# Block products added by accumulating transfers, a ring of product units, and a rearranged first block in a fused convolution and feed-forward kernel

## The chip, the cores and the metric

The kernel runs on one core of one Trainium2 chip. The core has five engines with a queue each, in order: TensorE (PE: matmuls, which write PSUM), VectorE (DVE), ScalarE (ACT), GpSimd (POOL) and SyncE (SP, which here issues nearly all transfers). The metric is the device time of one execution in microseconds (us). In the profile, PEld is PE's weight load.

## The reference, cut to what matters

```
def A(q, k, v, shift_k, ssm_k, ssm_D):            # S = 2048, D = 640, bf16
    k_shift = sum over t<4 of k shifted by t along S, times shift_k[:, t]
    kv = k_shift * v
    y  = irfft(rfft(kv padded to 2S) * rfft(ssm_k padded to 2S))[:S]   # causal convolution along S
    y  = y + kv * ssm_D
    return q * y
def B(x): return (silu(x @ w_gate) * (x @ w_up)) @ w_down              # F = 1728
h   = x + A(layernorm(x), k, v, ...)              # x = A_q
out = h + B(layernorm(h))
```

## The kernel before

**Tiling.** The sequence is cut in four blocks of 512 rows (i = 0..3). The causal convolution becomes a sum over block pairs: block i of the spectrum is the sum over j <= i of X[j] * C[i-j], where X[j] is the transform of block j of kv and C[m] that of parts of the convolution kernel, combined by `kcomb`. So block 1 has two products, block 2 three, block 3 four.

**Stages of block i.** `kv`: kT is loaded transposed, the four taps run as matmuls on PE (L543, L548; 64-row and 64-column tiles with the tap weights on a diagonal), ACT copies the result back into kT (L554), five DMA transposes turn it to kvo, and DVE multiplies it into vt (L563). `xfwd` (via `halves`): 32 matmuls with cosine and sine tables (L502), ACT evicts them (L514), DVE butterflies (L491) make X. `prod(j, i)`: for each half f2 two DVE multiplies of 2560 elements (L576, L577) into the temporary tt, one subtraction and one addition (L579, L581) and, for j > 0, one addition into the sum Y (L584). After the last j, butterflies give IO and IE. `inverse`: 32 matmuls (L637); then, per column group j of 0..3, ACT adds a bias while it evicts (L648), DVE multiplies (L650), ACT sums and sums squares (L652, L654), POOL makes the norm's factor with a power (L656, L658), DVE scales (L660) and a DMA transpose brings the result to hnT. `ffn`: 13 full slots of gate and up matmuls (L681, L682: 10 each) and a half-filled slot (L692), in which gate and up take 64 rows each; ACT evicts with Silu and Copy (L699, L701), DVE multiplies to gu or gz (L703); then the down matmuls of each j (L715, 14 slots by two halves; gz's first 64 rows are zeros) and DVE's last addition (L721) before the store. Before that, kc is transposed on PE (L477) and copied by ACT (L482) to KT, and `kfwd` transforms it; for kf0 DVE evicts half of it with the butterfly in one operation (L510). The first norm of x is `ln1`: for block 0 by DVE's statistics (L598, L599), for others by ACT (L607, L610); ACT applies it (L622).

**Order.** Every operation is recorded with `add` as a task with a number; `schedule` takes a written order of these numbers for each engine (ORDER) and gives out four PSUM units of two banks each, and `emit` makes the waits. So nothing is reordered on the chip, and a wait holds all that stands behind it on its engine. IO shares its place with kT, and IE with hnT.

Of the kernel before, what the change touches and what calls it, by code (L numbers as in the profile page):

```python
# [10 lines left out]
ALU = mybir.AluOpType  # L11
ACTF = mybir.ActivationFunctionType
P = 128
# [10 lines left out]
class _Task:  # L24
    __slots__ = ("eng", "fn", "cost", "lat", "deps", "after", "succ", "npred", "ready", "end", "start",
                 "opens", "tiles", "idx", "clock", "sem", "seq", "dma", "name", "gap")


class _Tile:
# [8 lines left out]
    def f(self, b, n, parts=slice(0, P)):  # L38
        o = self.unit * 1024 + b * 512
        return self.g.ps[parts, o:o + n]  # L40

# [13 lines left out]
class _Graph:  # L55


    def __init__(self, nc, es, units=4):
        self.nc = nc
        self.es = es  # L60
        self.tasks = []
        self.lastw = {}
        self.readers = {}
        self.units = units
        self.ps = es.enter_context(nc.psum_tensor("ps", [P, 4096], dt.float32))
        self.psb = self.ps[:].bitcast(dt.bfloat16)
# [26 lines left out]
    def add(self, eng, name, fn, cost, r=(), w=(), pr=(), pw=(), skip=(), lat=None, dma=None, after=()):  # L93
# [4 lines left out]
        t.after = set(after)  # L98
        t.opens = None
        t.tiles = []  # L100
        t.gap = 0.0
        t.seq = len(self.tasks)
# [34 lines left out]
    def schedule(self, order):  # L137
# [17 lines left out]
        pipe = 0.0  # L155
        self.glob = []
        while len(self.glob) < len(self.tasks):
            best = None
            for e in ENGINES:
# [3 lines left out]
                s = max(free[e], t.ready)  # L163
                if t.opens is not None:
# [11 lines left out]
            if t.opens is not None:  # L176
                pt = t.opens
                u = min((u for u in range(self.units) if unit_by[u] is None), key=lambda u: unit_free[u])
                pt.unit = u
                left[pt] = len(pt.users)  # L180
                t.deps.update(last_users.get(u, ()))
                unit_by[u] = pt
            free[e] = s + t.cost
            t.end = s + t.cost + t.lat
# [19 lines left out]
    def emit(self, block):  # L204
# [5 lines left out]
        for t in self.glob:  # L210
            kn = known[t.eng]
            waits = {}
            merged = []
            for d in t.deps:
# [64 lines left out]
    """,  # L279
    "act": """  # L280
# [10 lines left out]
    """,  # L291
    "dve": """
# [10 lines left out]
    """,  # L303
    "pool": """
        8 5 6 7 147 148 149 150 151 204 205 196 220 197 221 212 213 327 328 329 408 409 400 384 401 392 385 393 506 507 508 581
        597 582 598 589 573 590 574 695 696 697 780 796 781 797 772 773 788 789
    """,
    "sp": """
# [7 lines left out]
def bass_sequential_preLN__ssm_conv_h3__swiglu_ffn__prompt_kernel(  # L316
# [31 lines left out]
    ftab_d = nc.inline_tensor(_to_bf16(np.stack([np.cos(angx), np.sin(angx)], 1).reshape(P, -1)), name="cst_ftab")  # L348
    itab_d = nc.inline_tensor(_to_bf16(np.stack([np.cos(angi), np.sin(angi)], 1).reshape(P, -1)), name="cst_itab")
# [4 lines left out]
    with ExitStack() as es:  # L354
# [16 lines left out]
        Y = sb("Y", S[6], [4, 2, D])  # L371
# [10 lines left out]
        tt = sb("tt", o, [2, 2, 2, D])  # L382
        t1, t2 = tt[:, 0], tt[:, 1]
        tacc = bass.AP(t1.tensor, t1.offset, [list(t1.ap[0]), [2 * D, 2], [5 * D, 2], [1, D]])
# [9 lines left out]
        jk = sb("jk", o + 15360, [D])  # L394
        ub = [sb("ub%d" % i, o + 16640 + 1024 * i, [N]) for i in range(2)]
        gz = sb("gz", o + 18688, [N])
        o += 19712
# [13 lines left out]
        KO = [sb("KO%d" % m, p, [2, 2, D]) for m, p in enumerate((w + 10240, S[4], w + 10240, S[4] + 5120))]  # L411
        o = w + 17920
# [4 lines left out]
        mv = [sb("mv%d" % i, o + 320 + 32 * i, [4], f32) for i in range(4)]  # L417
# [3 lines left out]
        BN, DIRECT = (0,), ('kf0',)  # L421
# [26 lines left out]
        load("ftab", ftab[:], ftab_d.ap().rearrange("p (a j c) -> p a j c", a=2, j=4), 524288)  # L448
        load("itab", itab[:], itab_d.ap().rearrange("p (a f j c) -> p a f j c", a=2, f=2, j=4), 524288)
# [5 lines left out]
        g.add("pool", "gz", lambda e: e.memset(gz[0:H, :], 0.0), 500, w=[gz[0:H, :]])  # L455
# [36 lines left out]

        def halves(cls, name, src, ev, od, scale, direct=False):
# [23 lines left out]
        def kfwd(m, dst):  # L517
            halves("kf", "kf%d" % m, KT[m], dst, KO[m], D ** 0.5 / N, "kf%d" % m in DIRECT)
            for f in range(0 if "kf%d" % m in DIRECT else 2):
                bfly("kf%d" % m, dst[:, f], KO[m][:, f], dst[:, f], dst[:, f + 2], 2 * D)  # L520

        def kcomb(dst, own, prev, m):
# [3 lines left out]
                  cdve(4 * D), r=[own[:, :, 1, :], prev[:, :, 0, :]], w=[dst[:, :, 1, :]])  # L526

        def kv(i):
# [6 lines left out]
            for a in range(3):  # L535
# [17 lines left out]
                ks = kT[:, c0:c0 + nb, 0:N]  # L553
                g.add("act", nm, lambda e, pt=pt, ks=ks, nb=nb: e.activation(  # L554
# [5 lines left out]
            for lo, src, n, k in ((0, 0, P, 3), (P, P + H, H, 2), (P + H, P, H, 2)):  # L560
# [4 lines left out]
        def xfwd(i):  # L565
            halves("xf", "xf%d" % i, vt, XH[i], FO, 1.0, "xf%d" % i in DIRECT)
            for f in range(0 if "xf%d" % i in DIRECT else 2):
                bfly("xf%d" % i, XH[i][:, f], FO[:, f], XH[i][:, f], XH[i][:, f + 2], 2 * D)

        def prod(j, i):  # L570
# [228 lines left out]
```

## Time and profile before

| | |
|---|---|
| median of 3 runs (lowest to highest) | 274.79 us (273.31 to 275.04) |
| the profiled execution: its own time | 276.58 us |
| span of the profile | 274.6 us |
| mean granted PE clock | 0.981 |
| PE busy | 255.8 us (93%) |
| DVE busy | 210.5 us (77%) |
| ACT busy | 187.9 us (68%) |
| POOL busy | 37.8 us (14%) |
| chain that ended last | PE 58%, DVE 25%, ACT 9%, DMA 6% |
| DVE: L576 and L577 | 20 each, 29.7 us each |
| DVE: L584 | 12 of 2560 elements, 17.8 us |

The page splits the span in 40 slices of 6.9 us; a digit is the busy share in tenths. Matmuls overlap in their records: a PE that is shown busy is not at its peak, and the pace is read from start to start. A row of the timeline gives start, duration, engine, line, operation, output and inputs, the count, and in brackets the idle time ahead with what ended it. In a row of stages each engine has its busy time in that stretch and, in brackets, its instructions; the last three columns are the granted PE clock, the DMA engines' share and GB/s.

### The profile page before, as it was taken

How to read it: one execution, taken by the hardware profiler on the slowest of the kernel's cores; microseconds unless marked ns; L12 is line 12 of the kernel's file. 1: busy time of each engine (PE TensorE's matmuls, PEld its weight loads, DVE VectorE, ACT ScalarE, POOL GpSimd, SP SyncE). 2: the span in 40 equal slices, each digit the busy share in tenths (PEclk: the TensorE clock that was granted, in tenths of full speed). 3: DMA queues.
4: the chain of work that ended last, by engine and by line, in shares of the span. 5: the costliest groups of instructions: out<-in, count | busy, mean ns of one | idle time of the engine just before them, and what ended most of it. 6: DMA issues, size and time to landing. Idle time of an engine off the chain costs nothing.

```text
span 274.6 us, 4036 instructions
## 1 busy us (share of the span) xinstructions
PE 255.8 (93%) x1596; PEld 143.4 (52%) x1596; DVE 210.5 (77%) x281; ACT 187.9 (68%) x338; POOL 37.8 (14%) x54
## 2 busy tenths in 40 slices
PE   0998767899899999999999999999999999999995
PEld 0566434354544566754444666644446774444673
DVE  1479997987999999999999999999999413212222
ACT  1798998989966799167978892667769911546400
POOL 1002302900040011100040054000500220000000
PEclk9999989599999999999999999999999999999999
DMA  7999974274900073463100415530000050200002
GB/s 171 318 175 319 381 272 98 48 118 102 376 17 0 0 169 85 94 170 114 46 1 2 98 21 124 143 98 0 0 0 2 1 121 2 72 0 2 0 24 72
DMA packets 45204, 26.49 MB, mean 96 GB/s; under 512 B 34945, under 2 KB 43906, under 8 KB 45186
## 3 DMA queue, kind: packets, MB, share of 16 engines
q1 hardware_dynamic: 44528, 26.23, 35.2%
q8 instruction: 12, 0.20, 0.3%
q10 hardware_dynamic: 658, 0.01, 0.1%
q14 instruction: 6, 0.05, 0.1%
HBM read 15.69 MB, written 2.62 MB: 67 GB/s over the span
## 4 chain that ended last, share of the span: by engine, by line
PE 58%; DVE 25%; ACT 9%; DMA 6%; SPq 1%; issue 1%; DVEq 0%
PE ps L681 16%; PE ps L682 16%; PE ps L715 11%; PE ps L502 6%; DVE tt L577 4%; DMA kvo<-kT 4%; DVE tt L576 4%; PE ps L637 3%; PE ps L548 2%; DVE X L491 2%; DMA ident<-cst_id 2%; DVE xh L721 2%; DVE vt L563 2%; PE ps L692 2%; ACT qo L648 2%; DVE Y L584 2%
## 5 line engine op out<-in xcount | busy, mean ns | idle before, releaser
L715 PE MATMUL ps<-Wd,gu 128*128 128x320 bf16 x416 | 59.6, 299 | 0.0
L681 PE MATMUL ps<-hnT,GA 128*128 128x512 bf16 x140 | 53.1, 379 | 0.2 <-ACT ub L701 0.2
L682 PE MATMUL ps<-hnT,UA 128*128 128x512 bf16 x140 | 53.1, 379 | 0.0
L701 ACT ACTIVATE ub<-ps 128x512 bf16<-128x512 f32 (+1 forms) x56 | 32.8, 596 | 25.5 <-PE ps L682 19.3
L715 PEld LDWEIGHTS ps<-Wd,gu 128*128 128x128 bf16 x416 | 40.5, 98 | 17.0 <-DVE gu L703 0.5
L681 PE MATMUL ps<-hnT,GB 128*128 128x512 bf16 x120 | 45.5, 379 | 0.0
L682 PE MATMUL ps<-hnT,UB 128*128 128x512 bf16 x120 | 45.5, 379 | 0.0
L699 ACT ACTIVATE gu<-ps 128x512 bf16<-128x512 f32 x52 | 30.1, 596 | 13.4 <-PE ps L682 13.2
L703 DVE TENSOR_TENSOR gu<-gu,ub 128x512 bf16<-128x512 bf16 x52 | 21.2, 420 | 23.3 <-ACT gu L699 14.0
L576 DVE TENSOR_TENSOR tt<-X,C 128x2560 bf16<-128x2560 bf16 x20 | 29.7, 1484 | 0.1
L577 DVE TENSOR_TENSOR tt<-X,C 128x2560 bf16<-128x2560 bf16 x20 | 29.7, 1484 | 0.1
L502 PE MATMUL ps<-KT,ftab 128*128 128x320 bf16 x128 | 21.7, 316 | 4.0 <-ACT KT L482 1.6
L721 DVE SCALAR_TENSOR_TENSOR xh<-ps,st,xh 128x640 bf16<-128x640 f32 x16 | 14.0, 879 | 14.4 <-PE ps L715 14.4
L681 PEld LDWEIGHTS ps<-hnT,GA 128*128 128x128 bf16 x140 | 13.7, 98 | 17.3 <-ACT ub L701 0.7
L682 PEld LDWEIGHTS ps<-hnT,UA 128*128 128x128 bf16 x140 | 13.7, 98 | 15.7
L514 ACT ACTIVATE FO<-ps 128x640 bf16<-128x640 f32 x16 | 10.7, 705 | 14.3 <-PE ps L502 14.3
L502 PE MATMUL ps<-vt,ftab 128*128 128x320 bf16 x128 | 18.8, 299 | 1.5 <-DVE vt L563 1.4
L682 PEld LDWEIGHTS ps<-hnT,UB 128*128 128x128 bf16 x120 | 11.8, 98 | 14.2
L681 PEld LDWEIGHTS ps<-hnT,GB 128*128 128x128 bf16 x120 | 11.8, 98 | 14.1
L502 PEld LDWEIGHTS ps<-KT,ftab 128*128 128x128 bf16 x128 | 11.5, 101 | 13.2 <-ACT KT L482 2.7
L656 POOL TENSOR_SCALAR mv<-mv 128x1 f32<-128x1 f32 x16 | 6.6, 418 | 85.5 <-ACT qo L654 85.5
L584 DVE TENSOR_TENSOR Y<-Y,tt 128x2560 bf16<-128x2560 bf16 x12 | 17.8, 1486 | 0.1
(73 smaller groups left out, 377.8 us busy)
## 6 DMA issues: line engine op xcount, KB each, us to landing
kc<-in_A_ssm_k_dram SPq DMA_DIRECT2D x4, 640.0 KB, 5.6
xh<-in_A_q_dram SPq DMA_DIRECT2D x4, 640.0 KB, 5.2
vt<-in_A_v_dram SPq DMA_DIRECT2D x4, 640.0 KB, 6.2
out_dram<-xh SPq DMA_DIRECT2D x16, 160.0 KB, 2.0
Wd<-in_B_w_down_dram SPq DMA_DIRECT2D x1, 1280.0 KB, 6.9
UA<-in_B_w_up_dram SPq DMA_DIRECT2D x1, 1120.0 KB, 10.3
GA<-in_B_w_gate_dram SPq DMA_DIRECT2D x1, 1120.0 KB, 14.6
UB<-in_B_w_up_dram SPq DMA_DIRECT2D x1, 960.0 KB, 10.7
```

What stands on the lines that cost most here:

```text
L502: last = e.matmul(pt.f(c, W), ftab[:, cs, j, f * P:(f + 1) * P], src[:, j, c * W:(c + 1) * W], start=(j == par), stop=(j == par + 2))
L514: g.add("act", name, lambda e, pt=pt, d=d: e.activation(out=d.rearrange("p (b x) -> p b x", b=2), in_=pt.f2(W), func=ACTF.Copy, scale=scal ...
L576: g.add("dve", nm, lambda e, x=x, k=k: e.tensor_tensor(out=t1, in0=x, in1=k, op=ALU.mult), cdve(2560), r=[x, k], w=[t1])
L577: g.add("dve", nm, lambda e, x=x, k=ksw: e.tensor_tensor(out=t2, in0=x, in1=k, op=ALU.mult), cdve(2560), r=[x, k], w=[t2])
L584: g.add("dve", nm, lambda e, yy=yy: e.tensor_tensor(out=yy, in0=yy, in1=tacc, op=ALU.add), cdve(2560), r=[yy, tacc], w=[yy])
L681: e.matmul(pt.f(0, N), wg[:, c, f0:f0 + P], hnT[:, c, :], start=(c == 0), stop=(c == NC5 - 1))
L682: last = e.matmul(pt.f(1, N), wu[:, c, f0:f0 + P], hnT[:, c, :], start=(c == 0), stop=(c == NC5 - 1))
L699: g.add("act", nm, lambda e, pt=pt, gv=gv, a=ps_g: e.activation(out=gv, in_=pt.f(a[0], N, a[1]), func=ACTF.Silu, scale=D ** 0.5), cact(N), ...
L701: g.add("act", nm, lambda e, pt=pt, uv=uv, a=ps_u: e.activation(out=uv, in_=pt.f(a[0], N, a[1]), func=ACTF.Copy, scale=D ** 0.5), cact(N), ...
L703: g.add("dve", nm, lambda e, uv=uv, gv=gv: e.tensor_tensor(out=gv, in0=gv, in1=uv, op=ALU.mult), cdve(N), r=[gv, uv], w=[gv])
L715: last = e.matmul(pt.f(c, W), slots[fb][:, j * P:(j + 1) * P], Wd[:, fb, c * W:(c + 1) * W], start=(fb == 0), stop=(fb == 13))
L721: g.add("dve", nm, lambda e, pt=pt, x2=x2, m=m: e.scalar_tensor_tensor(out=x2, in0=pt.f2(W), scalar=m, in1=x2, op0=ALU.subtract, op1=ALU.add),
```

## The change

- **Accumulating transfers** (ACC). For the pairs (j, i) = (1,2), (1,3) and (2,3), the addition into Y is no longer a DVE operation but a transfer from the product into Y that adds on its way, issued from POOL: six transfers of 640 KB.
- **Ring of units.** The temporary tt (four units of [2, D]) becomes T with five units; each half product pops four and returns them in an order in which the two that hold the product come last. Y is laid out by halves.
- **Block 0's taps** (PT). Instead of five DMA transposes, PE transposes kT with the identity and DVE multiplies vt with the result in PSUM.
- **Block 0's norm** (ST). DVE adds the bias, multiplies and sums in one operation from PSUM; POOL scales the sum; ACT does only the squares. The gain of block 0's feed-forward changes accordingly.
- **kf0** is evicted by ACT and combined by butterflies (DIRECT is empty).
- **Pairs** (PAIR). The half-filled slot's product is stored by halves of the rows (gz: 64 rows by 256, twice), w_down's last 64 rows are loaded twice, and the down matmuls of that slot run as 64-row matmuls on two row tiles, j with j + 2. The order of j is 0, 2, 1, 3.
- **Idle places.** 18 matmuls of zeros at the start (WARM), a Silu on two elements at the start, and filler matmuls into a unit that is opened later, where the written plan has PE idle for over 700 ns: 7 ahead of kf0, 6 ahead of the first feed-forward matmul.
- **ORDER** is another list, for all engines. On SP, ftab and the loads of kc, GA and vt come earlier; ACT's Silu copies and the places of DVE's products move.

Some branches of the diff are not taken (D8, R4 and BN2 are empty), and costs in the plan change; neither adds an instruction.

```diff
-        tt = sb("tt", o, [2, 2, 2, D])
-        t1, t2 = tt[:, 0], tt[:, 1]
+        T = sb("T", o, [NU, 2, D])                      # NU = 5
-        BN, DIRECT = (0,), ('kf0',)
+        BN, DIRECT, D8, PT, BN2, ST, R4, PAIR, WARM, ACC = (0,), (), (), (0,), (), (0,), (), True, 18, ((1, 2), (1, 3), (2, 3))
...
+            def spin(e, pt=pt):
+                for k in range(WARM):
+                    last = e.matmul(pt.f(k % 2, N // 2), z[:, 0:P], z, start=True, stop=True)
...
+                for _ in range(t.fill):
+                    prog["pe"].append(lambda e, t=t: e.matmul(t.opens.f(0, 192), self.warm[:, 0:P], self.warm, start=True, stop=True))
...
+                        for j in range(4):                                                # kv, i in PT
+                            for b in range(nb):
+                                src = kT[:, c0 + b, j:j + 509:4]
+                                last = e.matmul(tp.flat(P, P * (nb * j + b)), src, ident[:, 0:P] if b == 0 else iswap, start=True, stop=True)
...
+                    g.add("dve", nm, lambda e, tp=tp, d=d, nb=nb: e.tensor_tensor(
+                        out=d, in0=tp.flat(4 * P * nb).rearrange("p (j x) -> p j x", j=4), in1=d, op=ALU.mult), cps(4 * P * nb),
+                          r=[d], w=[d], pr=[tp])
...
+                u = [ring_t.pop(0) for _ in range(4)]                                     # prod
+                t1, t2 = pair(u[0], u[1]), pair(u[2], u[3])
+                out = [T[:, u[0]], T[:, u[2]]] if j else [y[:, 0], y[:, 1]]
...
+                ring_t.extend((u[1], u[3], u[0], u[2]))
                 if j:
-                    g.add("dve", nm, lambda e, yy=yy: e.tensor_tensor(out=yy, in0=yy, in1=tacc, op=ALU.add), cdve(2560),
-                          r=[yy, tacc], w=[yy])
+                    if (j, i) in ACC:
+                        g.add("pool", nm, lambda e, y=y1, z=z1: e.dma_start(y, z, accum_op=ALU.add, max_dma_last_dim=2560), 1100, r=[z, y], w=[y],
+                              dma=(2850, 0), lat=2500, lock=False)
+                    else:
+                        g.add("dve", nm, lambda e, y=y, z=z: e.tensor_tensor(out=y, in0=y, in1=z, op=ALU.add), cdve(2560), r=[y, z], w=[y])
...
+                if st:                                                                    # inverse, block 0
+                    g.add("dve", nm, lambda e, pt=pt, x2=x2, s=s, j=j, m=m: e.scalar_tensor_tensor(
+                        out=x2, in0=pt.f2(W), scalar=s[:, 3, j:j + 1], in1=x2, op0=ALU.add, op1=ALU.mult, accum_out=m[:, 4:5]),
+                          cps(D) + 120, r=[x, s[:, 3, j:j + 1]], w=[x, m[:, 4:5]], pr=[pt])
...
+                    def mm(e, j=j, ta=dn[j], tb=dn[j + 2]):                               # ffn, PAIR
+                        for c in range(2):
+                            for t, row, k in ((ta, H, j), (tb, 0, j + 2)):
+                                last = e.matmul(t.f(c, W), gz[row:row + H, k % 2 * P:(k % 2 + 1) * P], Wd[row:row + H, 13, c * W:(c + 1) * W],
+                                                start=(row == 0), stop=(row == H), tile_position=(row, 0))
```

In the changed kernel the addition that stays on DVE is L742, the transfer L739, the multiplies L729 and L730, sum and difference L733, the norm's product L812 and its square L817, the feed-forward L866 and L867, the down matmuls L910, and the pairs L922.

More of the change, by code (lines that the diff above doesn't have):

```diff
@@ L25 @@
     __slots__ = ("eng", "fn", "cost", "lat", "deps", "after", "succ", "npred", "ready", "end", "start",
-                 "opens", "tiles", "idx", "clock", "sem", "seq", "dma", "name", "gap")
+                 "opens", "tiles", "idx", "clock", "sem", "seq", "dma", "name", "gap", "lock", "fill", "late")
 class _Tile:
@@ L40, in f, with flat @@
         return self.g.ps[parts, o:o + n]
+    def flat(self, n, at=0):
+        o = self.unit * 1024 + at
+        return self.g.ps[:, o:o + n]
     def f2(self, n):
@@ L98, in add @@
         t.after = set(after)
+        t.lock = (eng == "pool" and bool(r) or eng == "dve" and not pr) if lock is None else lock
         t.opens = None
@@ L101, in add @@
         t.gap = 0.0
+        t.fill = 0
+        t.late = set()
         t.seq = len(self.tasks)
@@ L163, in schedule @@
                 s = max(free[e], t.ready)
+                if e == "pool" and t.lock and port:
+                    s = max(s, free["dve"] + 40)
                 if t.opens is not None:
@@ L180, in schedule @@
                 left[pt] = len(pt.users)
+                t.late = t.deps - set(last_users.get(u, ()))
                 t.deps.update(last_users.get(u, ()))
+                if self.warm is not None and e == "pe" and at[e] > 2:
+                    idle = s - max(free[e], unit_free[u])
+                    t.fill = int((idle - 250) / 83) if idle > 700 else 0
                 unit_by[u] = pt
             free[e] = s + t.cost
+            if e == "dve":
+                port = t.lock
             t.end = s + t.cost + t.lat
@@ L491, in bfly, with eighths, mm @@
                 g.add("dve", name, lambda e, d=d, op=op: e.tensor_tensor(out=d, in0=e_, in1=o_, op=op), cdve(n), r=[e_, o_], w=[d])
+        def eighths(cls, name, src, dst, scale):
+            for f in range(4):
+                for cs in range(2):
+                    pt = g.tile(cls)
+                    def mm(e, pt=pt, f=f, cs=cs):
+                        fs = slice((f % 2) * P, (f % 2 + 1) * P)
+                        for j in range(4):
+                            for c in range(2):
+                                tab = ntab[:, cs, j // 2, fs] if f > 1 and j % 2 else ftab[:, cs, j, fs]
+                                last = e.matmul(pt.f(c, W), tab, src[:, j, c * W:(c + 1) * W], start=(j == 0), stop=(j == 3))
+                        return last
+                    g.add("pe", name, mm, cpe(W, 8), r=[ftab[:, cs], src] + ([ntab[:, cs]] if f > 1 else []), pw=[pt])
+                    d = dst[:, f, cs, :]
+                    g.add("act", name, lambda e, pt=pt, d=d: e.activation(out=d.rearrange("p (b x) -> p b x", b=2), in_=pt.f2(W),
+                                                                         func=ACTF.Copy, scale=scale), cact(D), w=[d], pr=[pt])
         def halves(cls, name, src, ev, od, scale, direct=False):
@@ L520, in kfwd, with quarters, mm @@
                 bfly("kf%d" % m, dst[:, f], KO[m][:, f], dst[:, f], dst[:, f + 2], 2 * D)
+        def quarters(cls, name, src, ev, od, scale):
+            for r in range(4):
+                for cs in range(2):
+                    pt = g.tile(cls)
+                    def mm(e, pt=pt, r=r, cs=cs):
+                        for c in range(2):
+                            last = e.matmul(pt.f(c, W), ftab[:, cs, r, 0:P], src[:, r, c * W:(c + 1) * W], start=True, stop=True)
+                        return last
+                    g.add("pe", name, mm, cpe(W, 2), r=[ftab[:, cs], src[:, r, :]], pw=[pt])
+                    d = od[:, r // 2, cs, :] if r % 2 else ev[:, r, cs, :]
+                    g.add("act", name, lambda e, pt=pt, d=d: e.activation(out=d.rearrange("p (b x) -> p b x", b=2), in_=pt.f2(W),
+                                                                         func=ACTF.Copy, scale=scale), cact(D), w=[d], pr=[pt])
@@ L697, in ffn @@
                 slots.append(gt)
-                uv, gv = u[rows, :], gt[rows, :]
-                g.add("act", nm, lambda e, pt=pt, gv=gv, a=ps_g: e.activation(out=gv, in_=pt.f(a[0], N, a[1]), func=ACTF.Silu, scale=D ** 0.5),
-                      cact(N), w=[gv], pr=[pt])
-                g.add("act", nm, lambda e, pt=pt, uv=uv, a=ps_u: e.activation(out=uv, in_=pt.f(a[0], N, a[1]), func=ACTF.Copy, scale=D ** 0.5),
-                      cact(N), w=[uv], pr=[pt])
-                g.add("dve", nm, lambda e, uv=uv, gv=gv: e.tensor_tensor(out=gv, in0=gv, in1=uv, op=ALU.mult),
-                      cdve(N), r=[gv, uv], w=[gv])
-            for j in range(4):
-                pt = g.tile("dn")
+                parts = [(rows, ps_g, ps_u, slice(0, N))]
+                if fb == 13 and PAIR:
+                    parts = [(slice(H, P), ps_g, ps_u, slice(0, N // 2)), (slice(0, H), ps_g, ps_u, slice(N // 2, N))]
+                for rows, ps_g, ps_u, ts in parts:
+                    n = ts.stop - ts.start
+                    uv, gv = u[rows, ts], gt[rows, 0:n]
+                    g.add("act", nm, lambda e, pt=pt, gv=gv, a=ps_g, ts=ts: e.activation(out=gv, in_=pt.f(a[0], N, a[1])[:, ts], func=ACTF.Silu, scale=gain),
+                          cact(n), w=[gv], pr=[pt])
+                    g.add("act", nm, lambda e, pt=pt, uv=uv, a=ps_u, ts=ts: e.activation(out=uv, in_=pt.f(a[0], N, a[1])[:, ts], func=ACTF.Copy, scale=gain),
+                          cact(n), w=[uv], pr=[pt])
+                    g.add("dve", nm, lambda e, uv=uv, gv=gv: e.tensor_tensor(out=gv, in0=gv, in1=uv, op=ALU.mult),
+                          cdve(n), r=[gv, uv], w=[gv])
+            dn, pair = {}, ()
+            for j in ((0, 2, 1, 3) if PAIR else range(4)):
+                second = PAIR and j > 1
+                if not second:
+                    dn[j] = g.tile("dn")
+                pt = dn[j]
                 x = xh[i % 2][:, j, :]
@@ L767, in bass_sequential_preLN__ssm_conv_h3__swiglu_ffn__prompt_kernel @@
             ffn(i)
+        if WARM:
+            g.warm = ident[:]
         g.schedule(ORDER)
```

217 lines of the change are left out of this document (165 added, 52 removed), and 58 rows, old and new, of the table ORDER.

## The prediction

> **What bounds the kernel now.** First the page's row of slices.
>
> ```profile
> PE   0998767899899999999999999999999999999995
> ...
> DVE  1479997987999999999999999999999413212222
> ...
> PEclk9999989599999999999999999999999999999999
> ```
>
> TensorE (PE) is full from the ninth slice on; its holes, and the dips of its clock, lie in the first eight slices (6.9 us each). VectorE (DVE) is nearly full from slice 4 to slice 31. So I ask where the two depend on each other, in the chain of waits and the timelines of PE and DVE.
>
> ```profile
> 209.83 4.58 PE ps L637 x32
> 214.41 12.50 PE ps L715 x92
> 226.91 0.36 PE ps L681
> ...
> 256.19 15.23 PE ps L715 x112
> 271.44 0.88 DVE xh L721
> ```
>
> ```profile
> 59.96 0.39 PE L681 MATMUL ps<-hnT,GA 128*128 128x512 bf16 x1
> ```
>
> ```profile
> 26.17 2.42 DVE L491 TENSOR_TENSOR X<-X,FO 128x1280 bf16<-128x1280 bf16 x3 [0.19 <-ACT FO L514]
> ...
> 37.80 1.55 DVE L491 TENSOR_TENSOR IO<-Y 128x1280 bf16<-128x1280 bf16 x2
> ...
> 55.26 0.45 DVE L660 TENSOR_SCALAR qo<-xh,mv 128x640 bf16<-128x640 bf16 x1 [0.46 <-POOL mv L658]
> ```
>
> ```profile
> 208.12 1.55 DVE L491 TENSOR_TENSOR IO<-Y 128x1280 bf16<-128x1280 bf16 x2
> ```
>
> The first feed-forward matmul starts at 59.96. From there to the last matmul at 271.44 are 211.5 us, and PE's work in them is 210.6: 540 matmuls of 512 columns at 0.216 (five in 1.08), 448 L715 at 0.136 (112 in 15.23), 192 of L502 and L637 at 0.136, and the taps of blocks 2 and 3, 7.0. So PE has no idle time to give after 60; only an earlier start or less work helps. DVE is tied to the same end: block 3's IO is ready at 209.6 and PE takes it at 209.83. From there to the end of the span are 64.8 us, nearly all PE. Both paths must shorten.
>
> **The head.** Start-to-start on the timelines a DVE tensor_tensor of 2560 takes 1.40, of 1280 0.735, a 640 from PSUM 0.80; a ScalarE (ACT) eviction of 640 takes 0.59, a KT copy 1.2; ten PE transposes 0.64.
>
> Removed from block 0: five DMA transposes, which hold SP for 7.60 us from 11.48. Added: 20 PE transposes (1.3) and three DVE multiplies from PSUM, 2.9 by size from the 0.80 row, in place of 1.6. On PE 20 kf0 matmuls (2.7) now stand before the taps. Walked: ident lands at 6.2; ACT copies KT0 to 9.3; kf0 runs to 11.0, taps (32 at 0.083, 4 at 0.216) to 14.6, kT copies to 15.8; DVE's multiplies end at 18.2 (21.3 before). ACT then has seven evictions, two KT copies and 1.7 of waits for PSUM units, so that X's first half is ready at 24.1 (26.17 before). From there DVE does the same butterflies and product as before (13.1): IO at 37.4, 1.9 earlier. The kf0 evictions that left DVE (eight at 0.80 out, four 1280s in) lie in its earlier waits and gain no more here.
>
> Block 0's norm: per column group j the ACT eviction (0.79) and mean pass (0.92) go; a DVE product from PSUM that also sums (0.9, from 0.88) replaces a 0.40 one, and a POOL scale (0.42, L656's row) comes before ACT's square. The inverse of j = 0 waits for a PSUM unit until 43.0; its product ends at 46.5, its square, behind four evictions on ACT, at 49.0, POOL (0.42 + 0.98) at 50.4, DVE's scale at 51.2 (55.7 before), its transpose to hnT (2.6) at 54.0. Six filler matmuls in front cost up to 0.5. First feed-forward matmul: 54.5, 5.5 earlier. Ends: 52 if the waits for units that I counted don't come, 57 if PE's clock halves as here:
>
> ```profile
> 46.00:48.00 2.00, 0.03 (x1) 0.04 (x2) 1.97 (x2) 2.00 (x7) 1.58 (x2) 1.00 0.82 185
> 48.00:50.00 2.00, 1.01 (x4) 0.27 (x4) 1.99 (x3) 2.00 (x6) 2.00 (x3) 0.81 0.00 0
> 50.00:52.00 2.00, 1.96 (x8) 1.04 (x8) 1.98 (x3) 2.00 (x5) 2.00 (x3) 0.50 0.40 79
> ```
>
> After a 2.04 us hole PE (first busy column) is granted 0.50 of its clock (third last column). [...] The 18 warm-up matmuls lie in the wait for ident, which hides them: free. The Silu table load (1.28 at 62.83) moves to the start, into ACT's first wait. GA is loaded ahead of the last two kc blocks; 3.8 MB queue up to kc1, at 0.35 MB per us from 12.3 until 23.1; PE wants it at 24. Thin, but covered; if late, PE's K work slips beside the norm. Block 1's kT still shares IO's place, so on SP it waits for block 0's inverse as before, and block 0's hnT transposes stand behind it; it is issued about 40 and holds SP 2.70, well before the first hnT.
>
> **The pairs.** 32 zero-padded L715 matmuls (0.136 each, 4.35) become 32 of 64 rows, in pairs on two row tiles. Nearest row: the 64*64 taps, 16 in 1.33, 0.083 each. Taken: 2.66, a gain of 1.7, half of it before block 3's inverse; ends 0 (no overlap) and 2.2. The gz product splits in two on ACT and DVE (0.34 becomes 0.42 on DVE).
>
> **DVE.** Up to block 3's IO the count of instructions by kind falls from 188.8 to 180.2 us; after block 0's norm it is 147.9 before and 143.2 after (six Y additions of 1.40 out, three other 2560s moved in). From 55.7 to 209.6 before, 6.0 of waits came on top; I keep 5.0. So IO is ready at 51.2 + 143.2 + 5.0 = 199.4 plus S, the new stalls. PE gets there at 54.5 + 149.9 - 0.85 = 203.5. So 4 us of S cost nothing.
>
> **The accumulating transfers.** With five units and four per half product, the second multiply of the next half must wait until the transfer has read its unit. That wait stands on DVE; behind it queue the gu products, so ACT's ub buffers, so PE's PSUM units. In DVE's new order the work between a product's end and the wait is 6.7, 6.1, 6.0, 4.1, 4.8 and 6.5 us. With L the time from the product to the landing, S is the sum of L minus these. Nearest row, a load of the same size in a quiet stretch:
>
> ```profile
> xh<-in_A_q_dram SPq DMA_DIRECT2D x1, 640.0 KB, 4.0
> ```
>
> Some 2.1 of the 4.0 are movement. The accumulation also reads its target: 6.1 if that is as long again; POOL's issue taken as SP's 0.34: L = 6.44, S = 4.8. Ends: 4.4 (second read hidden; S = 0.3) and 10.1 (both reads and the write in turn, 1.9 for POOL; S = 26). POOL does slow down beside a busy DVE:
>
> ```profile
> 161.96 2.64 POOL L658 TENSOR_TENSOR mv<-mv,half 128x1 f32<-128x1 f32 x2
> ```
>
> 1.32 each, where DVE is full; in the idle stretch at 219.88 it is 0.57. POOL's other work behind these issues is two blocks' norms, with 20 us of room.
>
> [...]
>
> **Sum.** IO: the later of 203.5 and 204.2 (199.4 + 4.8). End: PE takes it 0.2 later, 204.4, and 64.8 less block 3's pairs (0.4) follow: 268.8 of span, against 274.6. (Block 2's pairs lie in the wait for block 3's hnT: 17.1 from 209.83 to 226.91 in the chain, which block 3's norm fills, and gain nothing.) The profiled execution took 276.58, 2.0 above its span; the median of the runs is 274.79, 0.2 above it. Forecast: 269.0.
>
> **Rivals.** *The transfers are slow* (slower). L over 7.4 makes S 10.2 and eats everything: 199.4 + 10.2 + 0.2 + 64.4 = 274.2. At L = 8, S = 13.8: 278; at 10.1, 290. For it: the POOL rows, and three covers below 6.1. Against: 4.0 for the plain load, and nearly idle DMA there. [...]
>
> *The head does not open.* FFN starts at 58 or later: ACT evictions or a halved clock keep hn late. Then PE sets the end: 58.5 + 149.05 + 64.4 = 272.0 or, with no pair gain, 273.2. For it: ACT was full in 28 to 56 too.
>
> *The head opens wider and L is short.* FFN at 50, S under 4: 50 + 149.05 + 64.4 = 263.5; DVE must then have finished the norm by 47. Against: the 13.1 us of product 0 stay.
>
> **How the numbers follow.** Within 1% (272.0 to 277.5) is about what a measurement can't tell from no change. Forecast, 265 to 272: 0.47. Wider head, below 265: 0.23. Head shut, 272 to 277.5: 0.13. Slow transfers, above 277.5: 0.17. Faster 0.70, same 0.13, slower 0.17. Below 262 I leave 0.06, above 278 0.14: range 262 to 278; the forecast case's own is 265 to 272.
>
> **What would show it.** First L866 matmul at 54.5; IO of block 0 at 37.4 and of block 3 near 204; DVE waits of up to 2.5 us at the second multiply of the half product after each transfer, the longest in product (2,3), none over 4; landing 6 to 7 us after issue; L922 at about 0.083; PE idle under 3 us after 54.5. Wrong would be: landing over 7.4, DVE idle over 10 us after 100, a first L866 after 57, or IO of block 0 after 39.

## The result and the profile after

The changed kernel takes 277.22 us (median of 8 runs, 276.72 to 278.14). The kernel before, run beside it, takes 274.92 (273.31 to 276.03). The ratio is 1.0103, with a 95% interval of 1.0079 to 1.0128: about 1% slower, where 269.0 was forecast. The profiled execution took 277.16, of which 275.4 are the span. Medians in this document are of all runs, while the ratios leave out a run that lies over 1.5% above the fastest of its kernel.

The same rows of slices as before, of the changed kernel:

```profile
PE   6997979799999999799999996989999999999995
...
DVE  1499899998999999999999996385999541202204
...
PEclk9999999999999999999999999899999999999999
```

The head is better filled and keeps its clock (1.00 in every stretch up to 60 us). But three holes have come to PE behind it, in slices 17, 25 and 27, and VectorE (DVE), which was full up to slice 31, has one of its own in slices 25 to 28, from 165 to 193 us. PE's timeline gives the first feed-forward matmul of blocks 0 to 2 and the one spectrum matmul that waited, with the wait in brackets:

```profile
53.87 0.38 PE L867 MATMUL ps<-hnT,UA 128*128 128x512 bf16 x1 [1.43 <-DMA hnT<-qo]
...
112.11 0.38 PE L867 MATMUL ps<-hnT,UA 128*128 128x512 bf16 x1 [1.44 <-DMA hnT<-qo]
...
170.46 0.38 PE L867 MATMUL ps<-hnT,UA 128*128 128x512 bf16 x1 [2.47 <-DMA hnT<-qo]
...
184.25 2.89 PE L566 MATMUL ps<-vt,ftab 128*128 128x320 bf16 x20 [1.36 <-DVE vt L700]
```

DVE's timeline gives block 0's IO and last norm scale, the four long waits of the later half, and block 3's IO:

```profile
35.21 1.55 DVE L537 TENSOR_TENSOR IO<-Y 128x1280 bf16<-128x1280 bf16 x2
...
49.47 0.44 DVE L844 TENSOR_SCALAR qo<-xh,mv 128x640 bf16<-128x640 bf16 x1
...
167.71 1.49 DVE L730 TENSOR_TENSOR T<-X,C 128x2560 bf16<-128x2560 bf16 x1 [2.09 <-DMA Y<-T]
...
177.57 0.43 DVE L893 TENSOR_TENSOR gu<-gu,ub 128x512 bf16<-128x512 bf16 x1 [3.79 <-ACT gu L889]
179.97 1.49 DVE L730 TENSOR_TENSOR T<-X,C 128x2560 bf16<-128x2560 bf16 x1 [1.98 <-DMA Y<-T]
...
190.01 1.49 DVE L730 TENSOR_TENSOR T<-X,C 128x2560 bf16<-128x2560 bf16 x1 [2.88 <-DMA Y<-T]
...
209.20 1.55 DVE L537 TENSOR_TENSOR IO<-Y 128x1280 bf16<-128x1280 bf16 x2
```

Feed-forward starts at 53.87 (59.96 before). Block 3's IO is there at 210.75 all the same (209.67 before). The chain of waits shows where the six microseconds went:

```profile
155.36 4.70 POOL mv L838 x2
160.06 0.50 POOL mv L842
160.56 7.13 DMA Y<-T
167.71 1.50 DVE T L730
...
170.36 9.59 DMA Y<-T
179.97 1.50 DVE T L730
...
182.62 7.36 DMA Y<-T
190.01 1.50 DVE T L730
...
209.28 1.48 DVE IO L537 x2
210.90 2.33 PE ps L798 x16
```

Before, the chain was DVE's own work in this stretch, but for one transpose of kvo, up to 192 us, and PE's from there on:

```profile
169.56 2.37 DMA kvo<-kT
171.95 0.96 DVE vt L563
...
192.26 0.61 ACT ub L701
192.91 0.39 PE ps L681
```

Now three of the six transfers stand in it with 24.1 us, and ahead of them a 4.70 us piece of two POOL instructions of one column each, of which the first was ready at 155.28. But DVE's path is not the only late one. What PE waited for after 52 us (us in total, times, longest; 1.4 of the first row are ahead of 53.87):

```profile
PE ps L867 <- DMA hnT<-qo: 5.3, 3, 2.5
PE ps L566 <- DVE vt L700: 1.4, 1, 1.4
...
PE ps L798 <- DVE IO L537: 0.4, 1, 0.4
```

For block 3's IO PE waited only 0.4 us: by its own holes it was as late as DVE.

### The profile page after: what moved, and what is told of

Read it like the earlier page. It is cut to its first block, busy times and chain, and to the rows that moved or that the text cites. A ratio compares the mean times of both kernels' runs of the same rounds, so it can differ in the third digit from the quotient of the medians.

```text
span 275.4 us, 4134 instructions
## 1 busy us (share of the span) xinstructions
PE 255.4 (93%) x1630; PEld 141.8 (52%) x1647; DVE 203.3 (74%) x280; ACT 183.4 (67%) x338; POOL 49.5 (18%) x63
## 4 chain that ended last, share of the span: by engine, by line
PE 41%; DVE 22%; DMA 15%; ACT 11%; POOL 5%; SPq 4%; issue 1%
PE ps L867 12%; PE ps L866 11%; PE ps L910 10%; DMA Y<-T 9%; DVE T L730 5%; DMA kc<-in_A_ssm_k_dram 5%; POOL mv L838 4%; PE ps L798 3%; DVE T L733 3%; DVE X L537 2%; DMA hnT<-qo 2%; DVE Y L742 2%; DVE T L729 2%; DVE gu L893 2%; ACT KO L578 2%; SPq L471 2%
## 5 line engine op out<-in xcount | busy, mean ns | idle before, releaser
L867 PE MATMUL ps<-hnT,UA 128*128 128x512 bf16 x140 | 54.1, 386 | 5.7 <-DMA hnT<-qo 5.3
L910 PE MATMUL ps<-Wd,gu 128*128 128x320 bf16 x416 | 59.1, 299 | 0.0
L866 PE MATMUL ps<-hnT,GA 128*128 128x512 bf16 x132 | 51.0, 387 | 0.0
L910 PEld LDWEIGHTS ps<-Wd,gu 128*128 128x128 bf16 x416 | 40.1, 98 | 17.6 <-issue 1.3
L866 PE MATMUL ps<-hnT,GB 128*128 128x512 bf16 x118 | 44.7, 379 | 0.6 <-ACT ub L891 0.5
L867 PE MATMUL ps<-hnT,UB 128*128 128x512 bf16 x118 | 44.7, 379 | 0.1
L730 DVE TENSOR_TENSOR T<-X,C 128x2560 bf16<-128x2560 bf16 x20 | 29.7, 1486 | 7.1 <-DMA Y<-T 6.9
L729 DVE TENSOR_TENSOR T<-X,C 128x2560 bf16<-128x2560 bf16 x20 | 29.6, 1482 | 0.0
L866 PEld LDWEIGHTS ps<-hnT,GA 128*128 128x128 bf16 x140 | 13.9, 99 | 22.6 <-DMA hnT<-qo 5.8
L838 POOL TENSOR_SCALAR mv<-mv 128x1 f32<-128x1 f32 x16 | 14.1, 883 | 55.0 <-ACT qo L836 51.9
L927 DVE SCALAR_TENSOR_TENSOR xh<-ps,st,xh 128x640 bf16<-128x640 f32 x16 | 13.8, 877 | 12.3 <-PE ps L910 12.3
L566 PE MATMUL ps<-KT,ftab 128*128 128x320 bf16 x128 | 20.5, 301 | 1.9 <-ACT R L578 0.7
L867 PEld LDWEIGHTS ps<-hnT,UA 128*128 128x128 bf16 x140 | 13.9, 99 | 16.1 <-issue 1.1
L866 PEld LDWEIGHTS ps<-hnT,GB 128*128 128x128 bf16 x120 | 11.7, 98 | 15.2 <-ACT ub L891 1.0
L733 DVE TENSOR_TENSOR T<-T 128x1280 bf16<-128x1280 bf16 x24 | 19.3, 819 | 0.3
L867 PEld LDWEIGHTS ps<-hnT,UB 128*128 128x128 bf16 x120 | 11.7, 98 | 13.8
L566 PEld LDWEIGHTS ps<-vt,ftab 128*128 128x128 bf16 x128 | 11.9, 98 | 9.0 <-DVE vt L700 1.9
L781 ACT ACTIVATE xh<-xh,st 128x640 bf16<-128x640 bf16 x16 | 14.8, 930 | 1.5 <-POOL st L777 1.5
## 6 DMA issues: line engine op xcount, KB each, us to landing
GA<-in_B_w_gate_dram SPq DMA_DIRECT2D x1, 1120.0 KB, 10.7
```

What stands on the lines that cost most here:

```text
L566: last = e.matmul(pt.f(c, W), ftab[:, cs, j, f * P:(f + 1) * P], src[:, j, c * W:(c + 1) * W], start=(j == par), stop=(j == par + 2))
L729: g.add("dve", nm, lambda e, x=x, k=k, t1=t1: e.tensor_tensor(out=t1, in0=x, in1=k, op=ALU.mult), cdve(2560), r=[x, k], w=[t1])
L730: g.add("dve", nm, lambda e, x=x, k=ksw, t2=t2: e.tensor_tensor(out=t2, in0=x, in1=k, op=ALU.mult), cdve(2560), r=[x, k], w=[t2])
L733: g.add("dve", nm, lambda e, p=p, q=q, d=d, op=op: e.tensor_tensor(out=d, in0=p, in1=q, op=op), cdve(1280), r=[p, q], w=[d])
L781: g.add("act", nm, lambda e, j=j, xj=xj: e.activation(out=xj, in_=xj, func=ACTF.Identity, scale=s[:, 4, j:j + 1], bias=s[:, 5, j:j + 1]), ...
L838: g.add("pool", nm, lambda e, m=m, bn=bn, st=st: e.tensor_scalar(out=m[:, 2:3], in0=m[:, 1:2], scalar1=LN_EPS * D ** 3 if st else LN_EPS i ...
```

## The experiments

Theory T: the transfers of pairs (1,3) and (2,3) last too long for the work that covers them. Theory H: a DVE that never pauses holds POOL's small instructions up, which keeps norms and hnT late. Rival O: the new places in the order are bad by themselves. A number such as 751 is that of the task in ORDER. "IO" is the end of block 3's IO on DVE, "FFN 2" the first feed-forward matmul of block 2, both from the profiled execution. The kernels of rows 2 to 12 ran in three groups: rows 2, 3 and 7 and the tail on one chip, then rows 5 and 8 to 10, and last rows 4, 6, 11 and 12, both on another chip. The median of the kernel before was 274.95, 274.04 and 274.95 beside them, so ratios of different groups can differ by 0.3% for this alone. The kernels of the last two groups also put the waits of one instruction into a fixed order, and no run has that alone.

| kernel | transfers | us | ratio to before (95%) | IO | FFN 2 |
|---|---|---|---|---|---|
| changed | 6 | 277.22 | 1.0103 (1.0079 to 1.0128) | 210.8 | 170.5 |
| all additions on DVE | 0 | 275.63 | 1.0056 (1.0019 to 1.0093) | 208.5 | 171.9 |
| pair (1,2) alone | 2 | 273.75 | 0.9948 (0.9915 to 0.9980) | 206.0 | 169.4 |
| the same and 746 | 3 | 275.26 | 1.0000 (0.9965 to 1.0036) | 207.7 | 171.1 |
| the same and 751 | 3 | 278.27 | 1.0113 (1.0052 to 1.0174) | 209.7 | 169.6 |
| the same and 761 | 3 | 274.90 | 1.0003 (0.9967 to 1.0040) | 206.1 | 169.7 |
| changed, small instructions between | 6 | 277.83 | 1.0103 (1.0063 to 1.0142) | 211.3 | 170.8 |
| changed, two exchanges | 6 | 276.25 | 1.0055 (1.0022 to 1.0088) | 207.6 | 170.2 |
| changed, vt's load early | 6 | 275.31 | 1.0034 (0.9999 to 1.0069) | 209.0 | 170.5 |
| pair (1,2), two exchanges | 2 | 273.76 | 0.9989 (0.9958 to 1.0021) | 206.3 | 169.7 |
| pair (1,2), tuned order | 2 | 272.14 | 0.9892 (0.9857 to 0.9926) | 205.0 | 167.9 |
| tuned order and 761 | 3 | 272.75 | 0.9924 (0.9892 to 0.9957) | 204.3 | 167.6 |

**Which additions.** The additions that go back to DVE leave POOL's list in ORDER and stand in DVE's right behind their product (552 behind 550, 746 behind 745, and so on). With pair (1,2) alone, ACC holds the halves (1, 2, 0) and (1, 2, 1):

```diff
-        ACC = ((1, 2), (1, 3), (2, 3))
+        ACC = ()
...
-                    if (j, i) in ACC:
+                    if (j, i, f2) in ACC:
```

> The changed kernel with all six additions back on DVE, each right behind its product. They cost DVE 6 x 1.40 = 8.4 us and take away its three waits for transfers (2.09 + 1.98 + 2.88 = 6.95). Theory T (the loss is the transfers' length): block 3's IO at 209.3 + 8.4 - 6.95 = 210.8, and up to 3.8 earlier if the wait for gu at 173.8 goes as well: 207 to 211, time 273 to 279, so no worse than the changed kernel's 277.2. Theory H (the loss is POOL held up by a DVE without a gap, which keeps the norms of blocks 1 and 2 late): the additions make DVE fuller, L838 still has instructions of 4 us and more, PE still waits over 2 us for hnT, 279 to 282. Rival O (neither: the places in the new order alone are bad): first FFN matmuls of blocks 1 and 2 no earlier than 112.1 and 170.5, whatever the transfers do.

> Only pair (1,2) is added by transfers (two of them, for which DVE did not wait); (1,3) and (2,3) are added by DVE: 4 x 1.40 = 5.6 us more on DVE than in the changed kernel, and the three waits of 6.95 us gone. Theory T: 2.8 us faster than with all additions on DVE, block 3's IO at 204 to 208, time 271 to 276. Theory H: POOL's holds at 96 and 155 us stay, PE waits for hnT as before, 275 to 279, but still some 2.8 below all additions on DVE. Rival O: as for all additions on DVE.

Against all additions on DVE, the two transfers of (1,2) save 1.9 us. The four others, added to these, cost 3.5 (273.75 to 277.22), although they take 5.6 us of work off DVE. So T holds for these four taken together. L838 still took 5.86 us in both kernels, and block 1's first feed-forward matmul still came at 112.81 and 111.74, against 112.11: H alone does not make the loss. O has this much: with all additions on DVE the kernel is no faster than before either (ratio 1.0056), since DVE then has as much to do as before, and PE waits 5.5 us in all between 60 and 212 us (0.9 before, 7.0 in the changed kernel, 4.1 with pair (1,2) alone). About half of PE's new waits are there without the four late transfers, then; the tuned order below has 1.7.

**One late transfer at a time.** Edit: pair (1,2) alone, and one half product more in ACC (746 and 751 are the halves of (1,3), 761 the second half of (2,3)). 756 was not tried alone.

> Transfers for pair (1,2) and for the second half of (1,3), the one that took 9.6 us; the other three additions on DVE. It saves DVE 1.40 us. Theory T: its landing takes 7 to 9.6 us again, because a load of vt, three stores and four DMA transposes of kvo are under way, against a cover of 4.1; DVE waits 2 us or more (its wait for gu included), the kvo transposes take over 3.5 us (2.5 without it), vt and block 3's spectrum come later: 274.2 to 276. Rival (only the late transfers together, or POOL's hold ahead of them, made them slow): landing at 6 us or less, 272.5 to 273.7.

> Transfers for pair (1,2) and for the first half of (1,3), which lies among block 2's four hnT transposes. It saves DVE 1.40 us against pair (1,2) alone (273.75). Theory T, in the form that the single transfer with 751 gave (a transfer pays only where no DMA transpose that something waits for lies beside it): landing 6.5 to 8 us, hnT transposes 3 us and more (2.6 without it), PE's wait for block 2's hnT 1.5 us or more (0.6), 274.5 to 277. Rival (751 was bad for the load of vt alone): landing under 6.5, hnT at 2.6, 273 to 274.

> Transfers for pair (1,2) and for the second half of (2,3), which has no other transfer beside it. Theory T: landing 5.6 us, DVE does not wait for it, block 3's IO 1.4 us earlier; PE, which sets the time of the kernel with pair (1,2) alone from block 2 on, gains nothing from that: 273.2 to 274. Rival (every late transfer costs, by POOL or by DVE's memory): 275 and more.

751 alone costs 4.5 us (273.75 to 278.27), three times what it takes off DVE. These are four runs: three took 278.1 to 278.6 at a mean clock of 0.994 or 0.993, and one, at 1.000, took 275.44. As much as 2.8 of the 4.5 may be the clock's, then; one run does not settle it. What lies beside the transfer shows where the hole behind this comes from. DMA issues from 169 to 181 us in the kernel with 751 (KB each, median us from issue to landing):

```profile
Y<-T POOLq DMA_DIRECT2D x1, 640.0 KB, 8.5
vt<-in_A_v_dram SPq DMA_DIRECT2D x1, 640.0 KB, 6.9
...
kvo<-kT SPq DMA_TRANSPOSE x4, 3.8
```

The same view with pair (1,2) alone:

```profile
vt<-in_A_v_dram SPq DMA_DIRECT2D x1, 640.0 KB, 4.7
...
kvo<-kT SPq DMA_TRANSPOSE x4, 3.4
```

(The 2.5 of the expectation leaves out the first of these four transposes.) The transfer is slow beside its neighbours and they are slow beside it: the longest of the transposes goes from 4.6 to 7.5 us. The hole on PE comes by DVE's order: DVE waits 2.00 us for the transfer and 2.18 for gu (1.17 without), and vt's multiplies, which stand behind, come at 181.60 (179.29), over 1 us after the last kvo has landed. PE stands still until 183.28 (PE's timeline with 751):

```profile
183.28 4.56 PE L566 MATMUL ps<-vt,ftab 128*128 128x320 bf16 x20 [2.26 <-DVE vt L700]
```

The 2.26 us hole is followed by 20 matmuls in 4.56 us, which took 2.89 in the changed kernel: the granted clock is 0.63 there.

746 slows block 2's hnT transposes (2.6 us to 4.5 in the median; PE's wait 2.51 in place of 0.60) and costs 1.5.

761 lands in 5.6 us with no other transfer beside it, and DVE does not wait for it; yet it costs 1.1 us, where T had it at 273.2 to 274 (the two intervals share only 0.9967 to 0.9980). IO ends at 206.1 as without it, because DVE then waits 1.14 us for block 3's ACT evictions instead, and PE begins block 3's inverse at 207.43 (206.39). The trace has the way there: three small POOL instructions of a norm (L772 to L777), beside a DVE stream that has shifted, take 4.89 us (3.66) and are done at 204.65 (203.09), ACT waits 1.56 us for them (0.32), its Silu ahead of the inverse starts at 206.79 (205.23), and PE waits 0.56 us for it (not at all without).

**Is POOL's hold the loss?** Small statistics instructions between DVE's (886 to 891, bn_stats of 64 columns; first diff), and, in another kernel, two exchanges that make DVE wait for its own result (second):

```diff
 "dve"
-        540 541 399 542 543 544 ... 742 743 744 745
+        540 886 541 887 399 542 543 888 544 ... 742 889 743 890 744 745 891
 "dve"
-        540 541 399 542 543 544 ... 742 743 744 745
+        540 542 541 399 543 544 ... 742 744 743 745
```

> The changed kernel with six small statistics instructions (64 columns each, about 0.13 us, nothing uses their result) put between DVE's two-input instructions around 96 and 155 us. Theory H: no L838 takes more than 1.7 us, the third transfer is issued by 159.5 (160.56 now), the first FFN matmul of block 1 comes by 111 and of block 2 by 168.7 (112.1 and 170.5), the clock stays at 1.00 there, DVE's 3.8 us wait for gu goes; time 272 to 275.5. Theory T: the transfers still last 7 to 9.6 us against covers of 4 to 6, the wait for gu becomes a longer wait for the transfer, time 276 to 278. If the long L838 have another cause than DVE, they stay at 4 us and more and nothing changes but 0.8 us of added work.

> The changed kernel with two pairs of DVE instructions exchanged in the order (in product (0,2) and in product (1,3), first halves): a sum or difference now stands right behind the multiply that it needs, so DVE pauses for a moment (1.52 us from start to start in place of 1.40) in the two stretches where one L838 took 5.86 and 4.7 us. Work is the same. Theory H (POOL is held as long as DVE runs without a pause, and that delay is the loss): no L838 over 1.7 us, the third transfer issued by 159.6 (160.56), block 1's first FFN matmul by 111.2 (112.11), 273.5 to 276. Theory T (the loss is the transfers of pairs (1,3) and (2,3), too long for their covers): the holds may go, but DVE's waits for transfers stay near 7 us in sum or grow, 276.5 to 278. If L838 stays long, the hold is not ended by such a pause and stays open.

> The kernel with transfers for pair (1,2) alone (273.75) and the two exchanges. There PE still waited 1.12 us for block 1's hnT and 0.60 for block 2's. Theory H for what is left: the first FFN matmul of block 1 by 111.0 (111.74), 272.2 to 273.2. If the hold costs nothing: 273.5 to 274.1.

The small instructions cut the first hold (5.86 to 1.19 us) and not the second (4.91), and the time stays (277.83). The exchanges end both. The instructions of L838 on POOL in the changed kernel (minimum, median and maximum in ns, then first and last start):

```profile
L838 POOL TENSOR_SCALAR mv<-mv x16: 201/223/5857, 41.7 to 223.4; 128x1 f32<-128x1 f32 x16
```

The same in the changed kernel with the two exchanges:

```profile
L838 POOL TENSOR_SCALAR mv<-mv x16: 210/340/1382, 42.2 to 220.4; 128x1 f32<-128x1 f32 x16
```

The third transfer then goes out at 159.84 in place of 160.56, but block 2's hnT is still late (PE waits 1.95 us) and the ratio falls from 1.0103 to 1.0055, with runs scattered from 273.9 to 278.4. In the profiled execution, one of the quickest of these (274.53), DVE waits only 2.4 us for transfers (6.95), where T had said near 7, but still 3.48 for gu; H had the third transfer out by 159.6 and block 1's feed-forward at 111.2, and they came at 159.84 and 112.36. In the kernel without the late transfers the exchanges change nothing (273.76 and 273.75). So H is real, and by the medians about 1 us of the 3.5: what it costs, it costs with the transfer that queues behind it.

**Contention or the memory?** A tail behind the changed kernel's last store with small POOL instructions and transfers, and block 3's load of vt moved away from the fourth transfer:

```diff
 "sp"
-        488 683 695 591 599 583 607 480 688 684
+        488 683 684 695 591 599 583 607 480 688
```

> The changed kernel with a tail behind its last store (the time of the whole says nothing; the output is left as it is). In the tail, one after another: two 128x1 scalars on POOL (a) alone, (b) beside six independent two-input DVE multiplies of 2560, (c) beside six that each wait for the one before, (d) beside six with a small statistics instruction between; then an accumulating transfer of 640 KB (e) alone, (f) beside eight such multiplies, (g) beside four DMA transposes, (h) beside a load of 640 KB, (i) beside all three. Theory H: (a) 0.2 to 0.4 us, (b) over 4 us, (c) and (d) under 1.7. [...] Theory T, by contention with other transfers: (e) 5.6 from issue to landing, (g) 7, (h) 7.4, (i) 9 or more; by DVE's use of the memory: (f) is the long one. If neither holds, all are 5.6 to 6.5.

> The changed kernel with block 3's load of vt issued right behind that of its kT (at some 150 us in place of 170.7), out of the way of the fourth transfer. Theory T by contention with other transfers: the fourth transfer lands in 7 to 8.5 us (9.6), time 275 to 276.8. If the transfer is long for another reason (its place behind POOL's scalars, DVE's use of the memory), it stays at 9 to 10 and the time at 277.

In the tail the transfer lands in 5.7 us alone, 5.6 beside eight DVE multiplies, 6.6 beside four DMA transposes, 6.7 beside a load, and 6.4 beside the transposes and the multiplies. (The load was to be there too, but SP issued it 5.0 us after the transfer.) DVE's two-input multiplies did not slow it (5.6 beside eight, 5.7 alone); other transfers did, by about 1 us in this still mild company, and by up to 4 in the kernel (9.6). With vt's load out of the way the fourth transfer lands in 6.8 us (9.6), and the time falls to 275.31 (T had 275 to 276.8). DVE waits 1.00 us for the fourth transfer and 2.01 for gu (1.98 and 3.79 in the changed kernel), and PE 0.39 us for vt (1.36). The wait for the fifth grows from 2.88 to 3.82.

**A version that beats both.** Pair (1,2) alone, with the exchanges, and with block 1's and block 2's norm scales and hnT transposes earlier:

```diff
 "dve"
-        540 541 399 542 543 544 292 388 546 412 545 404 547 396 549
+        540 542 399 396 541 543 412 544 292 388 404 546 545 547 549
-        742 743 744 745 746 577 601 476 590 747 598 479 582 749 606 748
+        742 744 743 577 601 745 476 590 746 598 479 582 606 747 749 748
 "sp"
-        489 498 493 497 494 389 413 405 397 293 501 303
+        489 498 397 493 413 497 389 405 494 293 501 303
```

> Transfers for pair (1,2) alone, and an order in which DVE's norm scales of blocks 1 and 2 and SP's hnT transposes come earlier (L838 not held, as with the exchanges). PE waited 1.12 and 0.60 us for hnT and 1.12 us for a PSUM unit that ACT's kT copy frees. If PE sets the time, its waits fall to under 1.5 us in sum and the time to 272 to 273; DVE has 1.3 us to give before it is the bound again. If another transfer takes their place (kvo), 273.5 to 274.5.

> The same with the second half of (2,3) by a transfer as well, so that DVE has 1.4 us more to give: if the kernel before it is held by PE alone, equal to it within 0.4 us; if by DVE, up to 1.4 us faster, 271.3 to 272.5.

272.14 us, 1.1% faster than before and 1.8% than the changed kernel. The 1.6 us under pair (1,2) alone come from the places in the order, which is the part that O has. PE's waits for hnT after the head shrink to one of 0.39 us. What PE waited for after 52 us with pair (1,2) alone (us in total, times, longest):

```profile
PE ps L867 <- DMA hnT<-qo: 3.1, 4, 1.1
PE ps L922 <- ACT kT L691: 1.1, 1, 1.1
PE ps L667 <- DMA kT<-in_A_k_dram: 0.8, 1, 0.8
```

And with the tuned order (the 1.7 are ahead of the first feed-forward matmul):

```profile
PE ps L867 <- DMA hnT<-qo: 2.1, 2, 1.7
PE ps L667 <- DMA kT<-in_A_k_dram: 0.7, 1, 0.7
```

With 761 as a transfer on top, DVE is done 0.6 us earlier and the kernel is 0.6 us slower (272.75; its quickest run is above the slowest without it), with the same 1.56 us wait of ACT for POOL and 0.56 of PE for ACT. So it is not DVE that holds the kernel there.

## Why the prediction was wrong

**The head** was right: IO of block 0 at 36.8 (37.4; the terms given, 24.1 and 13.1, make 37.2), norm at 49.9 (51.2), feed-forward at 53.87 (54.5), granted clock 1.00 throughout. The 54.5 took a full clock for granted: the head's longest hole was 1.43 us, and in the profile of before the clock was 0.50 behind one of 1.61 (39.41). From the norm to the feed-forward it took 4.0 us and not 3.3, so the hit within 0.6 is in part luck. **The pairs** were near: four L922 in 0.38 us, 0.095 each, not 0.083; 32 of them gain 1.3 us, not 1.7. **DVE's sum** was near too: 199.4 + 1.40 for each addition put back gives 207.8 and 205.0 for the kernels with none and two transfers, and IO came at 208.5 and 206.0.

**The step that failed is S**, the stalls on the transfers: 4.8 us by L = 6.44 for all six. The formula held, L did not. From the end of the product to the landing the trace gives 6.1, 5.9, 8.7, 9.9, 7.7 and 5.9 us. Against the covers 6.7, 6.1, 6.0, 4.1, 4.8 and 6.5 that is 2.7 + 5.8 + 2.9 = 11.4 us, and 199.4 + 11.4 = 210.8: the trace has 210.75. (Of the 5.8, 3.8 appear as the wait for gu, which comes first on DVE.) That it meets the trace to a tenth is luck: the norm was 1.3 early, the waits for transfers and that gu were 10.7 and not 11.4, and DVE's other waits 6.9 and not 5.0. I took L from a load in a quiet stretch, and in quiet it is near: 5.9 to 6.1, of which 0.3 are before the issue. No run shows the 0.34 us in L for POOL's issue, nor the 1.9 of the upper end: the six issues took 1.19 to 1.40. But three of the transfers go out among hnT and kvo transposes, the load of vt, stores and the load of x. The profile of before shows most of these in that stretch, and the new order shows the rest: block 3's load of vt, issued at 128.03 before, comes at 170.70 (later, where the list of the change says that the loads of vt come earlier), and four of block 3's kvo transposes come behind hnT's. I looked for room on DVE alone.

**What the transfers do to the others** was not in the sum at all. "PE idle under 3 us after 54.5" became 7.8 (218.3 us up to the last matmul, 210.5 busy), with waits of 1.44 and 2.47 for hnT and 1.36 for vt. The single transfer 746 brings the late hnT of block 2 (2.51 in place of 0.60), by transposes that take longer; 751 brings the late vt, by DVE that waits for the transfer first (with the two exchanges vt's multiplies also waited 0.87 us for kvo). Much of the rest is there without any transfer (5.5 us of waits between 60 and 212 us). So PE's term, 203.5, failed as well: PE came to block 3's inverse 0.4 us before IO was there, at about 210.5, and a smaller S would have gained no more than that as long as PE's holes stayed.

**"POOL's other work, with 20 us of room"** was wrong as well. The room was there on POOL, but not when the transfer needed it: the product of the third transfer ended at 159.0, and POOL was held in L838 until 160.06, so 1.56 of the 8.7 lie ahead of the issue, against 0.3 for the others.

**From span to time** I added 0.2 us, the median less the profiled span. Time and span lie 1.8 apart in every run of the changed kernel, and 1.9 to 2.0 in those of before: the profiled execution of before (276.58) was simply a long one. Its mean clock of 0.981 comes from stretches before 60 us alone (1.00 from there on), while the runs of this kernel at 0.992 and more take 273.2 to 274.4. So some of the 6.1 us by which the feed-forward starts earlier were to be had from this execution only. The span was missed by 6.6 us, which is S on DVE's path and the holes on PE's; the other 1.6 of the 8.2 are this step.

**The rivals.** "The transfers are slow" came in, at the size that it gave (274 to 278 for L up to 8); by the number alone, 277.22 lies in the stretch that I had given to the shut head. What slowed them was not DVE's multiplies: beside eight of them the transfer took 5.6 us. Those have two inputs. One L844 scale, which has one tensor as input, runs beside the third issue (160.63), which took 1.26 us on POOL as the others did (1.19 to 1.40); no run has such scales beside a transfer alone. The hold of L838 was not one DVE instruction long: the 5.86 us ran over six of them.

**Open.** In the tail, two small POOL instructions took 0.39 us alone, 2.79 beside multiplies without a pause, 1.68 beside multiplies that wait for each other and 3.04 with small statistics between. H had over 4 for the second and under 1.7 for the last: beside the multiplies without a pause the two took as long as two of these (1.40 each), and in the kernel one L838 alone took 5.86. PE and ACT were idle in the tail, which may or may not matter. More units for the ring, so that no multiply waits for a transfer, were not tried: by the kernel's own bound (L448) 321 bytes per partition are left, and a unit takes 2560.

## What to carry to other kernels

Price a transfer by what else is under way when it goes out (here 5.6 us from issue to landing in quiet, 9.6 in company), and then price what it does to those others: above all to transposes that an engine is waiting for (2.6 to 4.5 us with 746). Work taken off a full engine is worth its duration only if the wait that comes with it is shorter; here the two of pair (1,2) passed that test, three others did not, and one was not tried alone. The simple way to know was to move them one by one. An engine that works in order hands its wait on: what stood behind DVE's wait, vt, became PE's hole (2.26 us with 751). Before adding a term, ask of which execution the profile is, and make the sum in spans.

## What the runs showed of the hardware

- PE's granted clock fell with some holes of 1.6 to 2.5 us and not with others: it fell behind the 2.47 us of the changed kernel and the 2.26 with 751, and stayed at 1.00 behind 2.51 us (746, vt's load early) and even 2.82 and 2.89 (small instructions between). Read by the microsecond, it was 0.67, 0.50, 0.50 and 0.62 from 171 to 175 us in the changed kernel, and 0.61, 0.50, 0.50 and 0.68 from 184 to 188 with 751; either way 1.7 us of full clock are lost. In the profile of before it fell to 0.50 twice: at 39.0 us, within a hole of 1.61 us, and at 49.2 us, within the second of two holes, of 2.04 and 1.04 us, with four matmuls between them.
- The granted clock also sorts the runs of the kernel before: of 27 beside the first experiments, those with a mean clock of 0.992 and more took 273.2 to 274.4 us and those at 0.98 took 276.0 and more. The changed kernel has no such spread: one of its eight runs had 0.999 and took 277.63.
- A POOL instruction on one column (L838) lasted 5.86 us beside a DVE that did not wait; with the two exchanges, where DVE waits for its own result (1.52 us from start to start, not 1.40), none lasted over 1.38. Both holds of the changed kernel ended right behind the start of a DVE addition that reads PSUM (L927, at 102.17 and 159.74).
